# Two full-row phases per chunk instead of three in a fused scan and gated-unit kernel on TensorE

## The chip, the cores and the metric

The kernel runs on one core of a Trainium2 chip. The core has a matrix engine (TensorE, PE in the profile), a vector engine (VectorE, DVE), a scalar engine (ScalarE, ACT), a general one (GpSimd, POOL) and an engine that only issues transfers (SyncE, SP). The engines run side by side and wait for each other on semaphores. On each engine the instructions run in the order in which they were built. TensorE writes into PSUM, eight banks of 512 float32 columns on 128 partitions.

The metric is device time in microseconds (us) for one execution, the median of several runs. A profiled execution is a separate run with the hardware profiler on.

## The reference, cut to what matters

A layer norm of x (2048 tokens, 448 features) feeds two branches, whose product is added to x.

```python
xn = _layernorm(x)
# branch A: a diagonal complex recurrence over the 2048 tokens
dt = exp(log_dt);  Lam_bar = exp(dt * Lam)
B_bar = ((Lam_bar - 1.0) / Lam)[:, None] * Bmat
Bu = einsum("bld,pd->blp", xn, B_bar)
for t in range(L):
    h = Lam_bar * h + Bu[:, t, :]          # 448 complex states
y = 2.0 * einsum("blp,dp->bld", hseq, Cmat).real + xn * Dskip
# branch B: a gated unit, 448 -> 1792 -> 448
g = xn @ w_gate;  u = xn @ w_up
m = (sigmoid(g) * u) @ w_down
out = x + y * silu(m)
```

## The kernel before, in words

The tokens are cut into four chunks of 512, each of four tiles of 128. All weights stay on chip. For a chunk c the work is this:

- `prepare(c)`: normalize the four tiles on ScalarE (L456), turn them by transfers into the layout with features on partitions (`xnT`), and multiply the skip term on VectorE (`skip_row`, L464, into `xd`).
- 14 projection steps (`gu_step`): for each seventh of the hidden size one gate step ("g") and one up step ("u"). A step is seven pairs of half-row matmuls (L690, L691), each on 64 of the 128 rows of the array, 512 columns wide, and fills a buffer `gu` of two banks. There are three of them. ScalarE takes the tanh of a gate step out (L704, into `sig`, two buffers), and VectorE takes an up step out and multiplies (L707, into `hF`). The factor between tanh and sigmoid is put right later, by the scale of the Silu.
- Input projections of the recurrence (`b_units`): two groups, for scan parts 0 and 1, and 2 and 3. A group begins with half-row pairs, can put other work in (`mid`), and goes on with full-row matmuls (L758, L761). ScalarE copies the result into `bus` (L769 to L777).
- The recurrence (`whole(c)`): VectorE rotates the inputs, runs the scans (L812, L844) and rotates back into `hT`, one of two by parity of the chunk.
- `down(c, j)`: 14 full-row matmuls for tile j (L873) into one of two accumulator banks `acc`, and a Silu on ScalarE (L879) into one of six buffers `g_t`.
- `yout(c, j)`: seven full-row matmuls (L898) into an accumulator bank, then three operations on VectorE (L904 adds the skip term and frees the bank, L906 multiplies with `g_t`, L908 adds x), and the store (L910). The output buffers `o_t` are three, the `xd` buffers twelve.

`down` and `yout` take the two accumulator banks in turn.

Half-row and full-row matmuls are two modes of the array. A stretch of full-row work between half-row steps is called a phase here. Before the change chunks 2 and 3 have three: one in each group of input projections (the group's `down` goes between its half-row pairs and its full-row matmuls, and one `yout` follows), and a third with two `down` and two `yout` before the last two projection steps. Chunk 1 has three as well, without a `yout` in the first two. The `down` are of the chunk before. The `yout` in the third phase are of the chunk before, those in the first two of the chunk before that.

The order comes from a planner (`Plan`, L74). Every operation is recorded with an engine, an assumed duration in us and the names of what it reads and writes (`add`, L85). TensorE's operations stay in the order in which they are recorded, so the sequence from L922 to L1051 is TensorE's. For the other engines `solve` (L138) works back from TensorE's times to a latest start for each, then forward to a planned start, and `emit` (L240) issues everything in order of planned starts. The assumed durations thus set the order on VectorE, ScalarE, GpSimd and SyncE, and waits are made from the real dependences. The layer norm's inverse root for later tiles runs on GpSimd in `chain` (L425 to L446).

Behind the last projection step come the remaining `yout` and the four `down` of chunk 3, which use the free `gu` banks in place of accumulators.

Of the kernel before, what the change touches and what calls it, by code (L numbers as in the profile page):

```python
# [13 lines left out]
ALU = mybir.AluOpType  # L14
# [14 lines left out]
EPS = 1e-5  # L29
# [25 lines left out]
def dve1(n):  # L55
    return 0.067 + n / 960.0
# [17 lines left out]
class Plan:  # L74
# [10 lines left out]
    def add(self, eng, cost, fn, r=(), w=(), dma=0, lat=None, chain=False, name="", rate=230e3):  # L85
        o = Op()
        o.idx, o.eng, o.cost, o.fn, o.dma, o.name = len(self.ops), eng, cost, fn, dma, name
        o.lat = LAT.get(eng, 0.0) if lat is None else lat
        o.pre, o.suc, o.rate = {}, [], rate
        o.slot = None  # L90
        if dma and eng != "POOL":
            o.slot, self.n_dma = self.n_dma, self.n_dma + 1
        o.start = o.end = None
        for k in r:
            if k in self.w:
                self._edge(self.w[k], o, True)
        for k in w:
            for q in self.r.get(k, ()):
                self._edge(q, o, False)
            if k in self.w:  # L100
                self._edge(self.w[k], o, True)
        for k in w:
            self.w[k] = o
            self.r[k] = []
        for k in r:
            if k not in w:
                self.r.setdefault(k, []).append(o)
        if chain or eng == "PE" or (eng == "DVE" and self.seq):
# [137 lines left out]
def kernel(  # L246
# [18 lines left out]
    V, A, G, T, Q = nc.vector, nc.scalar, nc.gpsimd, nc.tensor, nc.sync  # L265
# [56 lines left out]
    mv = sbt("mv", [NT, 2])  # L322
# [22 lines left out]
    add = pl.add  # L345
# [80 lines left out]
    def chain(t0, n):  # L426
        ts = range(t0, t0 + n)
        var, mean = mv[:, t0:t0 + n, 1:2], mv[:, t0:t0 + n, 0:1]
        sd, rs, nm, ve = (q[:, t0:t0 + n, :] for q in (sdb, rsd, nmr, veb))
        ks = lambda k: [(k, t) for t in ts]  # L430
        if t0 < TPC:
            add("ACT", 0.3, lambda: A.activation(sd, var, ACT.Sqrt, bias=epsc[:]), r=ks("mv") + ["sqrttab", "epsc"], w=ks("sd"))
            add("POOL", 0.15, lambda: G.tensor_copy(out=meanf[:, t0:t0 + n, :], in_=mean), r=ks("mv"), w=ks("mf"))
            add("DVE", 0.2, lambda: V.reciprocal(out=rs, in_=sd), r=ks("sd"), w=ks("rs"))
            return
        bc = lambda t: t[:].unsqueeze(1).to_broadcast((P, n, 1))
        add("POOL", 0.4, lambda: G.tensor_single_scalar(out=ve, in_=var, scalar=EPS, op=ALU.add), r=ks("mv"), w=ks("ve"))
        add("POOL", 1.0, lambda: G.tensor_tensor(out=sd, in0=ve, in1=bc(halfc), op=ALU.pow), r=ks("ve") + ["consts"], w=ks("sd"))
        if t0 == TPC:
            add("DVE", 0.2, lambda: V.reciprocal(out=rs, in_=sd), r=ks("sd"), w=ks("rs"))  # L440
            add("DVE", 0.16, lambda: V.scalar_tensor_tensor(out=nm, in0=mean, scalar=-1.0, in1=rs, op0=ALU.mult, op1=ALU.mult),
                r=ks("mv") + ks("rs"), w=ks("nm"))
            return
        add("POOL", 1.0, lambda: G.tensor_tensor(out=rs, in0=sd, in1=bc(negc), op=ALU.pow), r=ks("sd") + ["consts"], w=ks("rs"))
        add("POOL", 0.4, lambda: G.tensor_tensor(out=nm, in0=mean, in1=rs, op=ALU.mult), r=ks("mv") + ks("rs"), w=ks("nm"))
        add("POOL", 0.4, lambda: G.tensor_single_scalar(out=nm, in_=nm, scalar=-1.0, op=ALU.mult), r=ks("nm"), w=ks("nm"))  # L446
# [419 lines left out]
    def down(c, j, first=False, bank=None):  # L866
        key, d = bank if bank else (lambda a: (("acc", a), acc[a][:, 0:D]))(next_acc())
        js = slice(j * P, j * P + P)

        def f():  # L870
            for ft in range(FT):
                m, h = ft % 7, ft // 7
                T.matmul(d, lhsT=hF[c % 2][:, m, h, js], rhs=wd[:, ft, :], start=(ft == 0), stop=(ft == FT - 1))  # L873
        add("PE", 14 * 0.189 + (SW if first else 0), f, r=[("wd", 0), ("wd", 1)] + [("hF", c % 2, m) for m in range(7)], w=[key],
            name=f"d{c}.{j}")
        g = gt_n[0] % NGT
        gt_n[0] += 1
        gt_of[c, j] = g
        add("ACT", act(448), lambda: A.activation(g_t[g][:], d, ACT.Silu, scale=0.5), r=[key, "silutab"], w=[("gt", g)])  # L879
# [4 lines left out]
    def yout(c, j, first=False, banks=None, parts=((0, D),)):  # L884
        js = slice(j * P, j * P + P)
        t = c * TPC + j
        g = gt_of[c, j]
        o = o_n[0] % NO
        o_n[0] += 1
        q = t % NXD  # L890
        xq = xd[q][:]
        for pi, (c0, c1) in enumerate(parts):
            key, y = banks[pi] if banks else (lambda a: (("acc", a), acc[a][:, 0:D]))(next_acc())
            y = y[:, 0:c1 - c0]

            def f(y=y, c0=c0, c1=c1):
                for i, (hm, cm) in enumerate(K_ORDER):
                    T.matmul(y, lhsT=hT[c % 2][:, hm, js], rhs=cT[:, cm, c0:c1], start=(i == 0), stop=(i == 6))  # L898
            n = c1 - c0
            add("PE", 7 * (0.004 + n / 2400.0) + (SW if first else 0), f,  # L900
                r=cTk + [("hT", c % 2, p) for p in range(4)], w=[key], name=f"y{c}.{j}")
            ok = ("o", o, pi)
            od = o_t[o][:, c0:c1]
            add("DVE", dve1(n), lambda od=od, y=y, c0=c0, c1=c1: V.tensor_tensor(out=od, in0=y, in1=xq[:, c0:c1], op=ALU.add),  # L904
                r=[key, ("xd", q)], w=[ok])
# [76 lines left out]
    one(1, 0, "u")  # L982
    prepare(2)
    b_units(1, (0, 1), lambda: down(0, 0, True))
    for i in range(3, 6):
        gu_step(1, i, i == 3)
    b_units(1, (2, 3), lambda: down(0, 1, True))
    for i in range(6, 12):
        gu_step(1, i, i == 6)
    down(0, 2, True)  # L990
    yout(0, 0)
    down(0, 3)
    yout(0, 1)
    for i in range(12, 14):
        gu_step(1, i, i == 12)
    whole(1)

    for i in range(0, 4):
        gu_step(2, i)
    b_units(2, (0, 1), lambda: down(1, 0, True))  # L1000
    yout(0, 2)
    for i in range(4, 7):
        gu_step(2, i, i == 4)
    b_units(2, (2, 3), lambda: down(1, 1, True))
    yout(0, 3)
    prepare(3)
    for i in range(7, 12):
        gu_step(2, i, i == 7)
    down(1, 2, True)
    yout(1, 0)  # L1010
    down(1, 3)
    yout(1, 1)
    for i in range(12, 14):
        gu_step(2, i, i == 12)
    whole(2)

    for i in range(0, 4):
        gu_step(3, i)
    b_units(3, (0, 1), lambda: down(2, 0, True))
    yout(1, 2)  # L1020
    for i in range(4, 7):
        gu_step(3, i, i == 4)
    b_units(3, (2, 3), lambda: down(2, 1, True))
    yout(1, 3)
    for i in range(7, 12):
        gu_step(3, i, i == 7)
    down(2, 2, True)
    yout(2, 0)
    down(2, 3)
    yout(2, 1)  # L1030
    for i in range(12, 14):
        gu_step(3, i, i == 12)
    whole(3)

    yout(2, 2, True)
    yout(2, 3)
    free_banks = []
    for s in range(3):
        a = (gu_n[0] + s) % 3
        for i in range(2):  # L1040
            free_banks.append((("gub", a, i), gu[a][:, i, 0:D]))
        gate([("gu", a)], [("gub", a, 0), ("gub", a, 1)])
    for j in range(2):
        down(3, j, bank=free_banks[j])
    for j in range(2):
        yout(3, j)
    down(3, 2, bank=free_banks[2])
    yout(3, 2)
    down(3, 3, bank=free_banks[3])
    a = next_acc()  # L1050
    yout(3, 3, banks=[(("acc", a), acc[a]), free_banks[4]], parts=((0, 128), (128, 448)))  # L1051
# [36 lines left out]
```

## Time and profile before

| what | value |
|---|---|
| median of 5 runs | 188.86 us (188.12 to 190.43) |
| profiled execution | 188.17 us |
| its span, first to last instruction | 186.4 us |
| TensorE clock granted | full in every slice |
| share of the span, chain that ended last | PE 60%, DVE 21%, DMA 8%, ACT 4% |
| u evacuations, L707 on `sig` | 21, mean 1214 ns |
| scans, L812 | 18 with a carried state, mean 1276 ns |
| L904 | 15 whole tiles, mean 615 ns |
| Silu, L879 | 16, mean 540 ns |
| moved by transfers over the span | 13.43 MB, mean 72 GB/s |

The profile is taken in one execution. Its own time is 1.77 us over its span. Matmuls are pipelined, and their ends are modelled, so for TensorE the distance between starts tells more than the durations: two rows overlap by the part that is hidden. On VectorE, too, a row overlaps the next by some 0.08 us. In a row, the text in brackets is the idle time just before it, and what ended it. A buffer's number is left out in names.

### The profile page before, as it was taken

The page shows a single profiled execution, that of the slowest core. Times are in us where ns is not written, and L with a number is a line of the kernel's source. Part 1 is how long each engine was busy: PE and PEld are TensorE (multiplying, and loading weights), DVE is VectorE, ACT ScalarE, POOL GpSimd, SP SyncE. Part 2 cuts the span into 40 slices and gives each one's busy share as a digit, 9 for nine tenths or more (in the row PEclk, how much of TensorE's full clock was granted, in tenths as well). Part 3 has the DMA queues.
Part 4 walks back from the last instruction along what each step waited for, and adds up shares of the span by engine and source line. Part 5 has one row for each costly group of instructions (what it writes and reads, how often), then busy time and mean ns, then how long its engine had stood idle before and what let it go on. Part 6 is the DMA issues. An engine that isn't in the chain of part 4 may idle for free.

```text
span 186.4 us, 3512 instructions
## 1 busy us (share of the span) xinstructions
PE 180.6 (97%) x1375; PEld 88.0 (47%) x1375; DVE 167.8 (90%) x303; ACT 87.7 (47%) x124; POOL 35.5 (19%) x87
## 2 busy tenths in 40 slices
PE   7999999999999999999999999999999999999991
PEld 2674444564444444444445445444445445445550
DVE  3732999999998999999999999999999999999963
ACT  3449997943949942241557441234444421501020
POOL 7135462920078000000048410000000000000000
PEclk9999999999999999999999999999999999999999
DMA  5999999499200038200000343000000000001220
GB/s 139 268 217 214 196 182 201 80 269 195 100 4 0 0 77 74 49 0 4 0 2 0 77 102 70 0 28 0 25 4 0 25 25 28 0 5 48 74 77 25
DMA packets 30257, 13.43 MB, mean 72 GB/s; under 512 B 19744, under 2 KB 30240, under 8 KB 30240
## 3 DMA queue, kind: packets, MB, share of 16 engines
q1 hardware_dynamic: 28336, 12.05, 32.0%
q10 hardware_dynamic: 1808, 1.15, 2.5%
q8 instruction: 11, 0.18, 0.4%
q14 instruction: 6, 0.05, 0.1%
q0 software_dynamic: 96, 0.00, 0.0%
HBM read 6.77 MB, written 1.84 MB: 46 GB/s over the span
## 4 chain that ended last, share of the span: by engine, by line
PE 60%; DVE 21%; DMA 8%; ACT 4%; issue 3%; POOL 1%; SPq 1%; DVEq 0%
PE gu L690 24%; PE acc L873 13%; PE acc L898 10%; PE gu L873 6%; DVE hF L707 6%; DMA x_all<-in_A_x_dram 5%; PE gu L758 4%; DMA wG<-in_B_w_gate_dram 3%; DVE bst L423 2%; DVE wv L812 2%; DVE cT L659 1%; DVE ta L805 1%; DVE ta L826 1%; SPq L351 1%; DVE tb L806 1%
## 5 line engine op out<-in xcount | busy, mean ns | idle before, releaser
L690 PE MATMUL gu<-xnT,wG 64*128 64x512 bf16 (+1 forms) x231 | 46.2, 344 | 0.3 <-DVE xnT L491 0.3
L691 PE MATMUL gu<-xnT,wG 64*128 64x512 bf16 (+1 forms) x231 | 46.2, 344 | 0.0
L690 PE MATMUL gu<-xnT,wU 64*128 64x512 bf16 x196 | 46.0, 376 | 0.0
L691 PE MATMUL gu<-xnT,wU 64*128 64x512 bf16 x196 | 46.0, 376 | 0.0
L704 ACT ACTIVATE sig<-gu 128x1024 f32<-128x1024 f32 x21 | 21.4, 1023 | 28.6 <-PE gu L691 24.2
L873 PE MATMUL acc<-wd,hF 128*128 128x448 bf16 x168 | 33.8, 353 | 0.2 <-ACT g_t L879 0.2
L873 PEld LDWEIGHTS <-hF 128*128 128x128 bf16 x224 | 21.2, 98 | 22.6 <-issue 3.9
L690 PEld LDWEIGHTS <-wG 64*128 64x128 bf16 x231 | 21.0, 94 | 21.2 <-issue 2.8
L690 PEld LDWEIGHTS <-wU 64*128 64x128 bf16 x196 | 18.1, 94 | 23.3 <-issue 1.4
L707 DVE SCALAR_TENSOR_TENSOR hF<-sig,gu 128x1024 bf16<-128x1024 f32 x21 | 25.5, 1214 | 2.5 <-PE gu L691 1.3
L812 DVE TENSOR_TENSOR_SCAN wv<-c_r,st,z 128x512 bf16<-128x512 f32 x18 | 23.0, 1276 | 0.0
L898 PE MATMUL acc<-cT,hT 128*128 128x448 bf16 (+1 forms) x112 | 22.6, 344 | 0.0
L691 PEld LDWEIGHTS <-wG 64*128 64x128 bf16 x231 | 21.0, 94 | 0.0
L879 ACT ACTIVATE g_t<-acc 128x448 bf16<-128x448 f32 x12 | 6.5, 539 | 28.5 <-PE acc L873 28.5
L691 PEld LDWEIGHTS <-wU 64*128 64x128 bf16 x196 | 18.1, 94 | 0.1
L758 PE MATMUL gu<-xnT,bT 128*128 128x512 bf16 x72 | 16.9, 379 | 0.0
L898 PEld LDWEIGHTS <-hT 128*128 128x128 bf16 x119 | 11.3, 98 | 10.0 <-issue 0.4
L423 DVE BATCH_NORM_STATS2 bst<-x_all 128x6 f32<-128x448 bf16 x16 | 9.4, 614 | 7.1 <-DMA x_all<-in_A_x_dram 7.1
L769 ACT CAST bus<-gu 128x1024 bf16<-128x1024 f32 x12 | 12.0, 1003 | 2.9 <-PE gu L758 2.8
L456 ACT ACTIVATE xn<-x_all,nmr,rsd 128x448 bf16<-128x448 bf16 x12 | 8.8, 768 | 7.3 <-DVE xd L464 4.6
L873 PE MATMUL gu<-wd,hF 128*128 128x448 bf16 x56 | 11.1, 352 | 0.0
L904 DVE TENSOR_TENSOR o_t<-acc,xd 128x448 bf16<-128x448 f32 (+1 forms) x16 | 9.5, 595 | 1.5 <-PE acc L898 1.4
(135 smaller groups left out, 240.8 us busy)
## 6 DMA issues: line engine op xcount, KB each, us to landing
out_dram<-o_t SPq DMA_DIRECT2D x15, 112.0 KB, 1.7
wd<-in_B_w_down_dram SPq DMA_DIRECT2D x2, 784.0 KB, 5.1
x_all<-in_A_x_dram SPq DMA_DIRECT2D x3, 448.0 KB, 5.2
wU<-in_B_w_up_dram SPq DMA_DIRECT2D x2, 448.0 KB, 11.9
wU<-in_B_w_up_dram SPq DMA_DIRECT2D x2, 336.0 KB, 7.2
wG<-in_B_w_gate_dram SPq DMA_DIRECT2D x2, 224.0 KB, 5.8
wG<-in_B_w_gate_dram ACTq DMA_DIRECT2D x2, 224.0 KB, 6.0
xnT<-xn SPq DMA_TRANSPOSE x24, 2.4
```

What stands on the lines that cost most here:

```text
L423: add("DVE", 0.6, lambda: V.bn_stats(out=bst[b][:], in_=x_all[:, t, :]), r=[("x", t)], w=[("bst", b)])
L456: add("ACT", 0.65, lambda: A.activation(xn[b][:, 0:448], x_all[:, t, :], ACT.Identity, bias=nmr[:, t, :], scale=rsd[:, t, :]), r=[("x", t) ...
L690: T.matmul(gu[a][:, 0, ts], lhsT=w_[0:H, s, ms], rhs=x[0:H, s, ts], start=(s == 0), stop=(s == 6))
L691: T.matmul(gu[a][:, 1, ts], lhsT=w_[H:P, (s + 1) % 7, ms], rhs=x[H:P, s, ts], start=(s == 0), stop=(s == 6))
L704: add("ACT", act(1024), lambda: A.activation(th, gu[a][:], ACT.Tanh, scale=0.5), r=[("gu", a)], w=[tk])
L707: add("DVE", dve1(1024), lambda: V.scalar_tensor_tensor(out=ho, in0=th, scalar=1.0, in1=gu[a][:], op0=ALU.add, op1=ALU.mult), r=[("gu", a) ...
L758: T.matmul(gu[a][:, i, :], lhsT=bT[:, kt, i, pt * P:pt * P + P], rhs=x[:, 2 * kt, :], start=False, stop=(kt == 2))
L769: add("ACT", act(1024), lambda u=u, a=a: A.copy(out=bus[u][:], in_=gu[a][:]), r=[("gu", a)], w=[("bus", u)])
L812: dve(1.194, lambda k=k: V.tensor_tensor_scan(out=wv[:, k, :], data0=rb, data1=z[:, k, :], initial=(st[pt][:, k, :] if c else 0.0), op0=AL ...
L873: T.matmul(d, lhsT=hF[c % 2][:, m, h, js], rhs=wd[:, ft, :], start=(ft == 0), stop=(ft == FT - 1))
L898: T.matmul(y, lhsT=hT[c % 2][:, hm, js], rhs=cT[:, cm, c0:c1], start=(i == 0), stop=(i == 6))
L904: add("DVE", dve1(n), lambda od=od, y=y, c0=c0, c1=c1: V.tensor_tensor(out=od, in0=y, in1=xq[:, c0:c1], op=ALU.add), r=[key, ("xd", q)], w ...
```

## The change

In chunk 1, the two phases of the input projections take two `down` of chunk 0 each, and there is no `yout`. In chunks 2 and 3 each of the two phases takes two `down` of the chunk before and two `yout` of the chunk before that, in turn. The third phase is gone, and so the last seven projection steps of a chunk follow each other. All `yout` of chunk 0 stand in chunk 2, all of chunk 1 in chunk 3, and all of chunk 2 behind the last projection step, where before there were two. There the `yout` of chunk 2 now alternate with `down` of chunk 3. In `chain` two assumed durations on GpSimd change. No operation's computation changes. The diff, with the removed repetition for chunk 3 left out:

```diff
-        add("POOL", 0.4, lambda: G.tensor_single_scalar(out=ve, in_=var, scalar=EPS, op=ALU.add), r=ks("mv"), w=ks("ve"))
-        add("POOL", 1.0, lambda: G.tensor_tensor(out=sd, in0=ve, in1=bc(halfc), op=ALU.pow), r=ks("ve") + ["consts"], w=ks("sd"))
+        add("POOL", 0.6, lambda: G.tensor_single_scalar(out=ve, in_=var, scalar=EPS, op=ALU.add), r=ks("mv"), w=ks("ve"))
+        add("POOL", 1.4 if n == 4 else 1.0, lambda: G.tensor_tensor(out=sd, in0=ve, in1=bc(halfc), op=ALU.pow), r=ks("ve") + ["consts"], w=ks("sd"))
...
     b_units(1, (0, 1), lambda: down(0, 0, True))
+    down(0, 1)
     for i in range(3, 6):
         gu_step(1, i, i == 3)
-    b_units(1, (2, 3), lambda: down(0, 1, True))
-    for i in range(6, 12):
+    b_units(1, (2, 3), lambda: down(0, 2, True))
+    down(0, 3)
+    for i in range(6, 14):
         gu_step(1, i, i == 6)
-    down(0, 2, True)
-    yout(0, 0)
-    down(0, 3)
-    yout(0, 1)
-    for i in range(12, 14):
-        gu_step(1, i, i == 12)
     whole(1)
-
-    for i in range(0, 4):
-        gu_step(2, i)
-    b_units(2, (0, 1), lambda: down(1, 0, True))
-    yout(0, 2)
-    for i in range(4, 7):
-        gu_step(2, i, i == 4)
-    b_units(2, (2, 3), lambda: down(1, 1, True))
-    yout(0, 3)
-    prepare(3)
-    for i in range(7, 12):
-        gu_step(2, i, i == 7)
-    down(1, 2, True)
-    yout(1, 0)
-    down(1, 3)
-    yout(1, 1)
-    for i in range(12, 14):
-        gu_step(2, i, i == 12)
-    whole(2)
...
+    for c in (2, 3):
+        for i in range(0, 4):
+            gu_step(c, i)
+        b_units(c, (0, 1), lambda: down(c - 1, 0, True))
+        yout(c - 2, 0)
+        down(c - 1, 1)
+        yout(c - 2, 1)
+        for i in range(4, 7):
+            gu_step(c, i, i == 4)
+        b_units(c, (2, 3), lambda: down(c - 1, 2, True))
+        yout(c - 2, 2)
+        down(c - 1, 3)
+        yout(c - 2, 3)
+        if c == 2:
+            prepare(3)
+        for i in range(7, 14):
+            gu_step(c, i, i == 7)
+        whole(c)
+
+    yout(2, 0, True)
     yout(2, 1)
-    for i in range(12, 14):
-        gu_step(3, i, i == 12)
-    whole(3)
-
-    yout(2, 2, True)
-    yout(2, 3)
...
-    for j in range(2):
-        down(3, j, bank=free_banks[j])
-    for j in range(2):
+    down(3, 0, bank=free_banks[0])
+    yout(2, 2)
+    down(3, 1, bank=free_banks[1])
+    yout(2, 3)
+    down(3, 2, bank=free_banks[2])
+    for j in range(3):
         yout(3, j)
-    down(3, 2, bank=free_banks[2])
-    yout(3, 2)
     down(3, 3, bank=free_banks[3])
```

More of the change, by code (lines that the diff above doesn't have):

```diff
@@ L984 @@
     b_units(1, (0, 1), lambda: down(0, 0, True))
+    down(0, 1)
     for i in range(3, 6):
         gu_step(1, i, i == 3)
-    b_units(1, (2, 3), lambda: down(0, 1, True))
-    for i in range(6, 12):
+    b_units(1, (2, 3), lambda: down(0, 2, True))
+    down(0, 3)
+    for i in range(6, 14):
         gu_step(1, i, i == 6)
-    down(0, 2, True)
-    yout(0, 0)
-    down(0, 3)
-    yout(0, 1)
-    for i in range(12, 14):
-        gu_step(1, i, i == 12)
-    whole(1)
-    for i in range(0, 4):
-        gu_step(2, i)
-    b_units(2, (0, 1), lambda: down(1, 0, True))
-    yout(0, 2)
-    for i in range(4, 7):
-        gu_step(2, i, i == 4)
-    b_units(2, (2, 3), lambda: down(1, 1, True))
-    yout(0, 3)
-    prepare(3)
-    for i in range(7, 12):
-        gu_step(2, i, i == 7)
-    down(1, 2, True)
-    yout(1, 0)
-    down(1, 3)
-    yout(1, 1)
-    for i in range(12, 14):
-        gu_step(2, i, i == 12)
-    whole(2)
[L1017 to L1029, printed above, removed]
-    yout(2, 1)
-    for i in range(12, 14):
-        gu_step(3, i, i == 12)
-    whole(3)
-    yout(2, 2, True)
-    yout(2, 3)
+    whole(1)
+    for c in (2, 3):
[17 more added lines that the diff above has]
+    yout(2, 0, True)
+    yout(2, 1)
     free_banks = []
```

## The prediction

> **What bounds the kernel now.** I read the engine shares of the page first, then TensorE's rows in order of time, then the waits, then VectorE's rows at the end. The shares alone leave two candidates:
>
> ```profile
> PE 180.6 (97%) x1375; PEld 88.0 (47%) x1375; DVE 167.8 (90%) x303; ACT 87.7 (47%) x124; POOL 35.5 (19%) x87
> ```
>
> Here a rule speaks against the change. The Trainium skill, "Perfetto Trace Analysis", Identifying the Most-Contended Engine, says that matmul busy time is no measure of how near TensorE is to its limit, while for VectorE the busy share is a fair one. By the rule alone VectorE (90%) would be the bound, and time taken off TensorE would be worth nothing. So I look at distances between starts instead. TensorE's timeline around the third full-row phase of chunk 2 (start, duration, engine, line; L690 and L691 are the two half-row matmuls of a pair, L873 is `down`, L898 is `yout`):
>
> ```profile
> 108.94 0.38 PE L690 MATMUL gu<-xnT,wU 64*128 64x512 bf16 x1
> 109.15 0.38 PE L690 MATMUL gu<-xnT,wU 64*128 64x512 bf16 x1
> 109.46 2.82 PE L873 MATMUL acc<-wd,hF 128*128 128x448 bf16 x14
> 112.12 1.49 PE L898 MATMUL acc<-cT,hT 128*128 128x448 bf16 x7
> 113.45 2.81 PE L873 MATMUL acc<-wd,hF 128*128 128x448 bf16 x14
> 116.09 1.49 PE L898 MATMUL acc<-cT,hT 128*128 128x448 bf16 x7
> 117.51 0.39 PE L690 MATMUL gu<-xnT,wG 64*128 64x512 bf16 x1
> ```
>
> Pairs start 0.215 us apart, so a projection step of seven pairs takes 1.51. A `down` takes 2.65, a `yout` 1.32. I laid these against every start from 75 us to the last matmul: there is no gap but the phase borders. The step before the phase takes 0.31 instead of 0.215 (109.15 to 109.46: 0.10 on entry), and the `yout` that ends it 1.42 instead of 1.33 (116.09 to 117.51: 0.09 on exit). So from 75 us on TensorE sets the end, the rule notwithstanding. The exception in chunk 1 is here:
>
> ```profile
> 68.76 1.49 PE L898 MATMUL acc<-cT,hT 128*128 128x448 bf16 x7
> 70.47 2.81 PE L873 MATMUL acc<-wd,hF 128*128 128x448 bf16 x14 [0.23 <-ACT g_t L879]
> ```
>
> This `yout` takes 1.71 to the next start where 1.32 is its due: 0.39 lost, because `down(0,3)` needs the accumulator whose Silu (L879) stands on ScalarE behind a normalization (L456) that waits for VectorE:
>
> ```profile
> 69.23 0.76 ACT L456 ACTIVATE xn<-x_all,nmr,rsd 128x448 bf16<-128x448 bf16 x1 [1.41 <-DVE xd L464]
> 69.90 0.52 ACT L879 ACTIVATE g_t<-acc 128x448 bf16<-128x448 f32 x1
> ```
>
> VectorE is nearly as full: the waits that end its idle time after 62 us are a few of 0.2 to 0.4, each for the up projection that it evacuates next. Its rows at the end show how much room there is:
>
> ```profile
> 163.80 1.22 DVE L707 SCALAR_TENSOR_TENSOR hF<-sig,gu 128x1024 bf16<-128x1024 f32 x1 [0.41 <-PE gu L691]
> 170.04 0.68 DVE L829 TENSOR_TENSOR hT<-ta,tb 128x1024 bf16<-128x1024 bf16 x1
> 175.57 0.62 DVE L904 TENSOR_TENSOR o_t<-acc,xd 128x448 bf16<-128x448 f32 x1
> 177.03 0.62 DVE L904 TENSOR_TENSOR o_t<-acc,xd 128x448 bf16<-128x448 f32 x1
> 181.44 0.29 DVE L904 TENSOR_TENSOR o_t<-acc,xd 128x128 bf16<-128x128 f32 x1 [1.41 <-PE acc L898]
> ```
>
> The last scan output `hT` of chunk 3 is ready at 170.72, and `yout(3,0)` starts at 171.57: 0.85 to spare. Before the last tile VectorE waits 1.41.
>
> **The change part by part.** *Borders.* Chunks 1, 2 and 3 lose one full-row phase each; the half-row pairs of the input projections already open the other two. Three entries and three exits go: 3 x (0.10 + 0.09) = 0.57, all on the path. The Trainium skill prices this differently: "TensorEngine Tiling (Array Packing)", Key Properties, says a change of tiling mode drains TensorE, and "TensorE: Matmul & The Clock Gate", Single matmul latency, gives a drain of roughly 175 ns. Six of those are 1.05. I take the rows, 0.57, and keep 1.05 for the range.
>
> *The lost 0.39 in chunk 1.* `yout(0,0)` and `yout(0,1)` leave chunk 1. The two accumulators then serve four `down` alone, each takes the one that the last but one `down` left, and at least a `down` (2.65) lies between, so the Silu (0.54) is done in time. The 0.39 goes. What is late next there: nothing on TensorE, since chunk 1 runs eight projection steps in a row, and of these only the u steps need VectorE.
>
> *The eight steps in a row* (twelve with the next chunk's first four). A slot of the three `gu` buffers must be free two steps (3.02) after its step ends, and a u evacuation takes 1.13 from start to start. I laid the built VectorE order end to end by the starts of the rows (scan 1.20, wide products and sums 0.60, L904 0.53, L906 and L908 0.30, L464 0.30), from the first u evacuation of chunk 1 at 41.99, which stands in the same place. Chunk 1's next ones then fall 0 to 0.4 after their steps end; VectorE waits for TensorE there, not the other way. In chunks 2 and 3 a few stand behind scans and are 1.0 to 1.5 later, inside the 3.02, or, beside the input projections, later still but before the slot's turn. One place has only 1.5: the u step two before the second input projection. There VectorE arrives within 0.5 of the step's end in both chunks, as it did before (row at 137.10, slot taken at 138.33). Cost nothing; the cover is some 1 us of VectorE lead, and what exceeds it comes at full price.
>
> *`yout` a chunk later.* The scan output may now be up to a phase later, so VectorE's scans get slack; against that, `down` and `yout` alternate on two accumulators in both phases, and L904 must free one within the 2.65 of the `down` between. In my lay-out L904 is at its place at 87.5 for a `yout` that ends at 87.4, and at 102.4 and 130.2 VectorE waits for it: margin 2.0. The two stores that moved on SP's queue behind six transposes keep none waiting: the output buffer they free is wanted some 5 us later. ScalarE's Silu of `down(1,3)` waits on its queue for L906 of `yout(0,1)`, some 12 us after its matmuls; behind it stands the next chunk's first tanh, which has its input only then. Nothing.
>
> *POOL's planned costs* (0.6 and 1.4 for 0.4 and 1.0) change no instruction, only places: VectorE takes the reciprocal L440, on which it idled 0.32, after a second L562, and L634 goes ahead of the third u evacuation. TensorE lost 0.33 at the first input projection (29.35; 0.76 to the next start where 0.43 is due), waiting for the fifth u evacuation that ended at 29.74; laid out anew it ends at 29.1. But L634 needs a transfer that POOL's copies saw land near 24.9, just when it is its turn, and the table step behind follows later. Bounds: 0.33 gained, 0.3 lost; I take 0.15 gained, as the larger of the two effects is off TensorE.
>
> *The tail.* Two more `yout` stand behind the last projection step: before `yout(3,0)` TensorE now has four `yout` and three `down`, 4 x 1.32 + 3 x 2.65 = 13.2. VectorE, from the last u evacuation on: 1.13, two scans 2.40, eight wide operations 4.83, L859 0.33, two L904 1.06, three L464 0.90, seven L906/L908 2.15, together 12.8, and 0.53 for the L904 that frees `yout(3,0)`'s accumulator, 13.3, and some 0.2 of latency at both ends. So `yout(3,0)` waits about 0.2: the 0.85 to spare is gone. From there VectorE needs 1.75, then 2.8 with the L904 of `yout(3,0)` in it, then two tiles of 1.46 (175.57 to 177.03), and reaches the last tile 20.8 after the last projection step; TensorE, with three `yout` and a `down` and the 0.60 from its end to L904 (180.84 to 181.44), also 20.8. The 1.41 is gone too, but nothing more is lost.
>
> Sum: -0.57 - 0.39 - 0.15 + 0.2 = -0.9. The profiled execution took 188.17, its span of 186.4 and 1.77 around it, so 187.3 for its like. It stands 0.69 under the median of 188.86; carried to the median, 188.0.
>
> **The rivals.** *VectorE is the bound after all.* Its work is the same and 0.9 less room leaves it no slack, so the end stays: 188.9. For it: 90% busy and the two margins that vanish. Against: the lay-out, where it waits 3 to 5 us in all for TensorE before the tail. *Slower: accumulators starve TensorE.* Where VectorE is more than 2.0 late at the L904 between two `yout`, TensorE stands. Two such places in chunk 2, two in chunk 3 and the one before `yout(3,0)`: at one scan (1.2) too late in three of them, 3.6 - 0.9 = +2.7, 191.6. For it: VectorE's order is fixed by a plan whose costs are not those of the rows, so one late transfer shifts all behind it. Against: it decides only from 2.0 late, and the old order, with three such places, had no such wait. *More is gained:* the drain at the skill's 1.05, 0.39 and 0.33, with no wait at the tail, 1.77, and the spread of the runs on top: 186.9. *That it isn't done:* TensorE's order is the program's own, and the built one has two phases a chunk; excluded.
>
> **How the numbers follow.** Forecast, 188.0: 0.60. VectorE bound, 188.9: 0.12. Slower, 191.6: 0.16, nearly all past 190.75. More gained, 186.9: 0.12, taken as past 1%. About 1% is what a measurement of this kernel can tell from no change, as its five runs spread over 2.3 us. So faster 0.12, same 0.72, slower 0.16. The forecast's own range is 187.1 (1.77 gained) to 188.6 (switch saved, tail 0.5 worse). To leave out no more than 2 in 10 it reaches to 186.9 below and, past the bound case, to 190.0 above.
>
> **What would show it.** Right: TensorE's rows have two full-row stretches in chunks 1 to 3, borders of 0.10 and 0.09 each; no wait for L879 near 66 us; the last projection step ends 3.6 us earlier than 163.6; `yout(3,0)` starts near 173, within 0.5 of the last L829. Wrong: rows of `yout` or `down` that start more than 0.3 after the step before, with L904 as releaser; a projection step that waits for L707; a bus copy (L769) late behind a normalization on ScalarE; or the scans of chunk 3 ending after 174.

## The result, and the profile after

The changed kernel takes 187.77 us in the median (187.14 to 188.52), the kernel before 188.51 in the runs beside it. The ratio is 0.9963, with a 95% interval of 0.9951 to 0.9976. That is 0.70 us less (the two medians stand 0.74 apart); the prediction had 188.0 against 188.86, a ratio of 0.9955.

The engine shares of the page hardly move, and the span, first to last instruction, goes from 186.4 to 186.0. The profiled execution itself did not get shorter: it took 188.52, the slowest of the 36, with 2.52 outside its span where the one before had 1.77. In the runs of the kernel before beside the experiments the time outside the span is always 1.72 to 1.95. In the changed kernel it is above 2.1 in 6 of 36, up to 2.90. No instruction stands in that time, and what takes it is not shown. So what follows, which is read from traces, is about the span alone.

What did move is the page's chain that ended last. The page's engine shares, then the chain's shares of the span by engine and by line:

```profile
PE 180.0 (97%) x1375; PEld 88.6 (48%) x1375; DVE 167.9 (90%) x303; ACT 87.8 (47%) x124; POOL 34.9 (19%) x87
...
DVE 4%; issue 1%; DVEq 0%
DVE o_t L904 2%; DVE o_t L906 1%; DVE xd L464 1%; DVE o_t L908 1%; DVEq L906 0%
```

Before, this chain was 60% TensorE. Now, followed back from the last instruction, it stays on VectorE. It ends after some 5% of the span and says nothing on what held TensorE before that, so it is a statement on the tail alone.

TensorE's timeline of the changed kernel, at the end of the second phase of chunk 1 and at the end of the second phase of chunk 2:

```profile
59.44 2.81 PE L873 MATMUL acc<-wd,hF 128*128 128x448 bf16 x14
62.18 0.39 PE L690 MATMUL gu<-xnT,wG 64*128 64x512 bf16 x1
...
105.04 1.49 PE L898 MATMUL acc<-cT,hT 128*128 128x448 bf16 x7
106.46 0.39 PE L690 MATMUL gu<-xnT,wU 64*128 64x512 bf16 x1
```

The `down` takes 2.74 to the next start, 2.65 and the 0.09 of a border. The `yout` takes 1.42, 1.33 and 0.09. Behind each, the half-row steps follow at 1.51 without a gap. Behind the first there are twelve in a row, from 62.18 to 80.32, at the place where chunk 1 had its third phase and its 0.39 of waiting.

The tail has changed sides. TensorE's timeline, then VectorE's, with the idle time before a row in brackets:

```profile
170.50 2.81 PE L873 MATMUL gu<-wd,hF 128*128 128x448 bf16 x14
173.47 4.13 PE L898 MATMUL acc<-cT,hT 128*128 128x448 bf16 x21 [0.16 <-DVE o_t L904]
177.44 2.81 PE L873 MATMUL gu<-wd,hF 128*128 128x448 bf16 x14
180.09 0.55 PE L898 MATMUL acc<-cT,hT 128*128 128x128 bf16 x7
```

```profile
172.21 0.68 DVE L829 TENSOR_TENSOR hT<-ta,tb 128x1024 bf16<-128x1024 bf16 x1
172.81 0.61 DVE L904 TENSOR_TENSOR o_t<-acc,xd 128x448 bf16<-128x448 f32 x1
173.34 0.38 DVE L464 TENSOR_TENSOR xd<-xn,dbc 128x448 bf16<-128x448 bf16 x1
173.81 0.62 DVE L904 TENSOR_TENSOR o_t<-acc,xd 128x448 bf16<-128x448 f32 x1
...
178.27 0.62 DVE L904 TENSOR_TENSOR o_t<-acc,xd 128x448 bf16<-128x448 f32 x1
...
179.73 0.62 DVE L904 TENSOR_TENSOR o_t<-acc,xd 128x448 bf16<-128x448 f32 x1
180.45 0.39 DVE L906 TENSOR_TENSOR o_t<-o_t,g_t 128x448 bf16<-128x448 bf16 x1
180.87 0.39 DVE L908 TENSOR_TENSOR o_t<-o_t,x_all 128x448 bf16<-128x448 bf16 x1
181.18 0.28 DVE L904 TENSOR_TENSOR o_t<-acc,xd 128x128 bf16<-128x128 f32 x1
...
182.85 0.32 DVE L908 TENSOR_TENSOR o_t<-o_t,x_all 128x320 bf16<-128x320 bf16 x1
```

The `down` at 170.50 takes 2.97 to the next start instead of 2.65. The accumulator of `yout(3,0)` comes free with the L904 that starts at 172.81 and ends at 173.42, so 0.32 is lost. Its `hT` was ready at 172.89, before TensorE would have come to it (173.15). And the last tile's L904 at 181.18 has no idle time before it. Before, VectorE waited 1.41 for TensorE there; now the matmuls are there first.

The two profiled executions, cut into stretches by starts on TensorE, with the end of the last L908:

| stretch | before | after | difference |
|---|---|---|---|
| to the first projection step | 7.92 | 8.11 | +0.19 |
| to the first half-row pair of chunk 1's input projections | 33.47 | 33.23 | -0.24 |
| to the end of the last projection step | 122.23 | 118.56 | -3.67 |
| to the narrow `yout` of the last tile | 17.22 | 20.19 | +2.97 |
| to the end of the last L908 | 2.76 | 3.08 | +0.32 |

Two `yout` (2.65) went from the third row to the fourth. Without them the third lost 1.02, and the fourth gained 0.32. All together is -0.43, and -0.62 without the first row. The ratio, which holds many executions, says -0.70.

### The profile page after: what moved, and what is told of

It is laid out like the page before. It is cut to its first block, busy times and chain, and to the rows that moved or that the text cites. A ratio compares the mean times of both kernels' runs of the same rounds, so it can differ in the third digit from the quotient of the medians.

```text
span 186.0 us, 3513 instructions
## 1 busy us (share of the span) xinstructions
PE 180.0 (97%) x1375; PEld 88.6 (48%) x1375; DVE 167.9 (90%) x303; ACT 87.8 (47%) x124; POOL 34.9 (19%) x87
## 5 line engine op out<-in xcount | busy, mean ns | idle before, releaser
L690 PEld LDWEIGHTS <-wG 64*128 64x128 bf16 x231 | 21.3, 94 | 20.9 <-issue 1.9
L707 DVE SCALAR_TENSOR_TENSOR hF<-sig,gu 128x1024 bf16<-128x1024 f32 x21 | 25.5, 1216 | 2.7 <-PE gu L691 2.0
L812 DVE TENSOR_TENSOR_SCAN wv<-c_r,st,z 128x512 bf16<-128x512 f32 x18 | 23.0, 1277 | 0.0
L691 PEld LDWEIGHTS <-wG 64*128 64x128 bf16 x231 | 21.2, 94 | 0.0
L879 ACT ACTIVATE g_t<-acc 128x448 bf16<-128x448 f32 x12 | 6.5, 538 | 26.1 <-PE acc L873 16.7
L423 DVE BATCH_NORM_STATS2 bst<-x_all 128x6 f32<-128x448 bf16 x16 | 9.3, 612 | 5.5 <-DMA x_all<-in_A_x_dram 5.5
L758 PEld LDWEIGHTS <-bT 128*128 128x128 bf16 x72 | 6.9, 98 | 8.5 <-issue 0.7
L437 POOL TENSOR_SCALAR veb<-mv 128x2 bf16<-128x2 bf16 (+1 forms) x5 | 2.5, 503 | 43.3 <-DVE mv L424 43.3
```

What stands on the lines that cost most here:

```text
L423: add("DVE", 0.6, lambda: V.bn_stats(out=bst[b][:], in_=x_all[:, t, :]), r=[("x", t)], w=[("bst", b)])
L690: T.matmul(gu[a][:, 0, ts], lhsT=w_[0:H, s, ms], rhs=x[0:H, s, ts], start=(s == 0), stop=(s == 6))
L691: T.matmul(gu[a][:, 1, ts], lhsT=w_[H:P, (s + 1) % 7, ms], rhs=x[H:P, s, ts], start=(s == 0), stop=(s == 6))
L707: add("DVE", dve1(1024), lambda: V.scalar_tensor_tensor(out=ho, in0=th, scalar=1.0, in1=gu[a][:], op0=ALU.add, op1=ALU.mult), r=[("gu", a) ...
L758: T.matmul(gu[a][:, i, :], lhsT=bT[:, kt, i, pt * P:pt * P + P], rhs=x[:, 2 * kt, :], start=False, stop=(kt == 2))
L812: dve(1.194, lambda k=k: V.tensor_tensor_scan(out=wv[:, k, :], data0=rb, data1=z[:, k, :], initial=(st[pt][:, k, :] if c else 0.0), op0=AL ...
```

## The experiments

All ratios are to the kernel before, which ran beside each. The changed kernel's own 0.9963 is what the variants of it are held against. A difference of 0.002 in the ratio is 0.38 us.

**The phases without the edit of the assumed durations, and the edit without the phases.** The first is the changed kernel with:

```diff
-        add("POOL", 0.6, ...
-        add("POOL", 1.4 if n == 4 else 1.0, ...
+        add("POOL", 0.4, ...
+        add("POOL", 1.0, ...
```

> The changed kernel with the old planned costs on GpSimd. Theory (TensorE sets the end up to the last projection step; the gain is 0.57 for six borders and 0.39 for the Silu wait): the borders and the Silu wait stay gone, only the 0.23 us at the first input projection may come back, so 0.4 to 0.8 us under the kernel before. Rival (the gain comes from the new places that the planned costs give in the first 40 us): no gain over the kernel before.

Measured: 188.19 us, ratio 0.9994 (0.9970 to 1.0018). The point lies outside what was expected (0.9957 to 0.9979); the interval reaches into it. The second is the kernel before with the new numbers.

> The kernel before with the new planned costs alone. Theory: at most the 0.33 us wait at the first input projection goes, so 0 to 0.3 us under the kernel before, with all three phases and their borders in place. Rival (planned costs): the whole gain, some 0.7 us.

Measured: 188.25 us, ratio 0.9996 (0.9976 to 1.0015). So neither half shows a gain by itself, while both together do, though the intervals of the first half and of the whole change touch. The traces suggest why. In the first, TensorE's stretch from the first pair of chunk 1 to the narrow `yout` is 138.77, as in the changed kernel (138.75; 139.45 before), and the end behind it is 3.10, also as there (3.08; 2.76 before). But TensorE reaches chunk 1's first pair 34.06 after the first projection step, where the changed kernel needs 33.23 and the kernel before 33.47. TensorE's timeline of this variant at the first input projection:

```profile
29.13 0.38 PE L743 MATMUL gu<-xnT,bT 64*128 64x512 bf16 x1
29.81 0.37 PE L743 MATMUL gu<-xnT,bT 64*128 64x512 bf16 x1 [0.30 <-DVE hF L707]
30.14 2.12 PE L758 MATMUL gu<-xnT,bT 128*128 128x512 bf16 x9
```

The second pair waits for an evacuation, L707, and 1.01 pass to the full-row matmuls where 0.53 is due (two pairs at 0.215 and the entry of 0.10). In the second variant the same place takes 1.12, while the wait for the Silu in chunk 1 is gone without any change of phases there, because VectorE and ScalarE are planned anew.

**The front of the new plan with the back of the old one.** To tell whether those 0.4 were lost in front, the order of all engines up to the first input projection was taken from the changed kernel's plan, and everything behind it from the plan with the old durations:

```diff
     pl.solve({"g0.0": 5.9})
+    T0 = next(o.start for o in pl.ops if o.name == "bp0.0") + 0.1
+    first = {o.idx: o.start for o in pl.ops if o.start < T0}
+    for o, cost in recost:
+        o.cost = cost
...
+    pl.solve({"g0.0": 5.9})
+    for o in pl.ops:
+        o.start = first[o.idx] if o.idx in first else o.start + 1000.0
```

> The phases of the change, with the order of all engines taken from the plan with the new GpSimd costs up to the first input projection, and from the plan with the old costs behind it. It differs from the phases with the old costs alone (ratio 0.9994) only in VectorE's, ScalarE's and GpSimd's order ahead of 30 us. If the 0.42 by which that one stood above the changed kernel was lost in front of the first input projection, this one is at the changed kernel's 0.996. If it was lost behind it, or by chance of the runs, it stays at 0.999.

Measured: 187.83 us, ratio 0.9973 (0.9950 to 0.9996). It lies between the two, nearer to the changed kernel; its interval holds both. In its trace the first input projection takes the due 0.53, and chunk 1's first pair comes 33.34 after the first projection step. But in that execution the load of chunk 1's x tiles also landed earlier than in the one with the old durations (tables at the end), so this trace alone does not tell the order from the landing. The time leans to the front and does not settle it.

**The Silu's wait, taken out another way.** The kernel before, with the third phase of chunk 1 as `down`, `down`, `yout`, `yout`:

```diff
     down(0, 2, True)
-    yout(0, 0)
     down(0, 3)
+    yout(0, 0)
     yout(0, 1)
```

> The kernel before, with the third phase of chunk 1 in the order down, down, yout, yout in place of down, yout, down, yout: same work, same borders, but the Silu that frees the accumulator has 2.65 us in place of 1.32. Theory: the 0.39 us wait at 70 us goes and the end comes 0.4 us earlier, since from there on TensorE has no gap. Rival (VectorE is the bound): TensorE's wait goes and the end stays.

Measured: 189.11 us, ratio 1.0031 (1.0017 to 1.0045): slower. The wait went, as expected; the two `down` now take 5.31, twice 2.65. But no gain came, which neither the theory nor its rival had; the planner had moved VectorE's order everywhere, and the trace shows new waits. TensorE's timeline of this variant:

```profile
30.88 0.37 PE L743 MATMUL gu<-xnT,bT 64*128 64x512 bf16 x1 [0.96 <-DVE hF L707]
...
62.55 0.37 PE L690 MATMUL gu<-xnT,wG 64*128 64x512 bf16 x1 [0.21 <-ACT bus L777]
```

The row at 62.55 is a projection step that waits for a copy on ScalarE (0.37 by distances), where there was none, and from chunk 1's first pair to the narrow `yout` the stretch is 139.45 as before. In this trace a wait's gain was taken out behind 40 us and put back by another one there. The row at 30.88 is no fair sample: this execution took 190.38, 1.27 over its median, and the load of the x tiles landed late in it (tables at the end). Part of the wait is the new order's, and what the 0.6 of the medians is made of is not shown.

**More borders.** In chunks 2 and 3 one projection step goes into the middle of each phase of the changed kernel:

```diff
         yout(c - 2, 0)
-        down(c - 1, 1)
+        gu_step(c, 4, True)
+        down(c - 1, 1, True)
         yout(c - 2, 1)
...
```

> The changed kernel with one projection step set between the first yout of each phase of chunks 2 and 3 and the down behind it: same work, four full-row phases per chunk in place of two, so four more pairs of borders. Theory: four times 0.19, 0.76 us over the changed kernel, so level with the kernel before. Rival (VectorE is the bound): as the changed kernel, 0.7 us under the kernel before.

Measured: 188.68 us, ratio 1.0006 (0.9987 to 1.0024): 0.8 us over the changed kernel, level with the one before. In its trace every added `yout` takes 1.42 and every added step 1.61. From chunk 1's first pair to the narrow `yout` it is 139.28; the changed kernel's 138.75 without its wait of 0.32 is 138.43. So eight more borders cost 0.85 on TensorE, where the rows' price of 4 x (0.10 + 0.09) is 0.76. The 0.8 of the time is another matter, and that it meets the 0.76 is luck as far as the trace goes. There VectorE had caught up when the tail began: `yout(3,0)` does not wait, and the tail from the last projection step to the end of the last L908 is 22.63, 0.64 shorter than the changed kernel's 23.27. So 0.21 of the 0.85 is left at the end. The rest of what this execution lost, 0.95, was lost before chunk 1's first pair (34.18 after the first projection step against 33.23), where the load of the x tiles landed later and VectorE's order is another.

**Two more VectorE copies in the tail.** The same two copies of 0.30 were put behind the L904 of `yout(2,3)`, in both kernels:

```diff
-            add("DVE", dve1(n), lambda ...: V.tensor_tensor(out=od, in0=y, in1=xq[:, c0:c1], op=ALU.add),
+            add("DVE", dve1(n), lambda ...: (V.tensor_tensor(out=od, in0=y, in1=xq[:, c0:c1], op=ALU.add),
+                V.tensor_copy(out=ctmp[0][:], in_=spm[:, 0, 0, 0:448]) if (c, j) == (2, 3) else None,
+                V.tensor_copy(out=ctmp[1][:], in_=spm[:, 0, 1, 0:448]) if (c, j) == (2, 3) else None),
```

> The kernel before with two extra copies on VectorE (some 0.3 us each) behind the L904 of the last tile of chunk 2, with results that nobody reads. Theory: VectorE waits 1.41 us before the last tile there, so the 0.6 us are hidden and the time is that of the kernel before. Rival (VectorE is the bound): 0.6 us more.

> The changed kernel with the same two extra copies at the same place. Theory: VectorE has no idle time left behind that place, so the full 0.6 us: level with the kernel before or 0.1 under. Rival (TensorE holds the end): 0.7 us under the kernel before, as the changed kernel.

Measured: in the kernel before 188.79 us, ratio 0.9997 (0.9968 to 1.0025), and in the changed one 188.28 us, ratio 0.9988 (0.9967 to 1.0010), 0.5 over the changed kernel. VectorE's timeline of the first, and TensorE's of the second:

```profile
182.94 0.29 DVE L904 TENSOR_TENSOR o_t<-acc,xd 128x128 bf16<-128x128 f32 x1 [0.81 <-PE acc L898]
```

```profile
174.40 2.81 PE L898 MATMUL acc<-cT,hT 128*128 128x448 bf16 x14 [0.16 <-DVE o_t L904]
177.57 1.49 PE L898 MATMUL acc<-cT,hT 128*128 128x448 bf16 x7 [0.37 <-DVE o_t L904]
```

Before, the 0.60 came out of the 1.41 of idle time: 0.81 is left, and from the last projection step to the end of the last tile it is 19.98, to the hundredth what it was without the copies. In the changed kernel `yout(3,2)` waits for VectorE, and the same stretch is 23.87 against 23.27: the whole 0.60. Of all traces this pair says most plainly that the bound of the tail has changed. The times agree with it and do not prove it, since the interval of the second touches the changed kernel's.

**Four skip products less.** The skip products of the last four tiles are left out of the changed kernel, so the outputs of chunk 3 are made with the skip term of chunk 0:

```diff
-        add("DVE", dve2(448), lambda: V.tensor_tensor(out=xd[q][:], ...),
+        add("DVE", dve2(448), lambda: V.tensor_tensor(out=xd[q][:], ...) if t < 12 else None,
```

> The changed kernel without the skip product of the last four tiles (four L464 of 0.30 us on VectorE, three of them behind the last scan output; leaves out that part of the computation: the tiles of chunk 3 read the skip term of chunk 0), all else at its place. Theory (the tail is now VectorE's by 0.3 to 0.5 us): the end comes 0.4 to 0.5 us before the changed kernel's, then TensorE holds it; 1.1 to 1.2 us under the kernel before. Rival (VectorE is the bound all along): the full 1.2 us, 1.9 under. Rival (TensorE holds the end): nothing more than the changed kernel, 0.7 under.

Measured: 187.11 us, ratio 0.9897 (0.9852 to 0.9941). VectorE's timeline of it:

```profile
180.17 0.29 DVE L904 TENSOR_TENSOR o_t<-acc,xd 128x128 bf16<-128x128 f32 x1 [0.63 <-PE acc L898]
```

VectorE waits for TensorE again, and the tail is 22.95 from the last projection step to the end of the last L908, against 23.27: the 0.32 of the table's last row. The wait of `yout(3,0)` stays at 0.31, since the products left out come behind it. The time is another matter. The ratio, 1.9 us under the kernel before, is better than the trace can explain; by itself it is what the rival had, for which VectorE is the bound all along. But it comes from six runs, and its interval reaches from 1.1 to 2.8 us under the kernel before, so that the theory's 1.1 to 1.2 lies at its edge. In the trace, where VectorE waits at the end and only 0.32 is gained, it is the theory that holds.

**The products of chunks 2 and 3 on GpSimd.**

```diff
+        if t < 8:
             add("DVE", dve2(448), lambda: V.tensor_tensor(out=xd[q][:], ...),
+        else:
+            add("POOL", 1.1, lambda: G.tensor_tensor(out=xd[q][:], ...),
```

> The changed kernel with the skip product of chunks 2 and 3 (eight L464) on GpSimd in place of VectorE. Theory: 2.4 us less on VectorE, five of the eight behind the last projection step, so both the wait of yout(3,0) of 0.3 us and the 0.4 us at the end go: 1.3 to 1.4 us under the kernel before. Rival: GpSimd takes over 2 us for one or slows VectorE's two-input operations beside it, and nothing is gained over the changed kernel.

Measured: 190.08 us, ratio 1.0083 (1.0057 to 1.0108): slower. The tail did what was wanted: 19.88 from the last projection step to the narrow `yout`, without a wait. But that step ended at 162.20 instead of 159.90. GpSimd's, VectorE's and TensorE's timelines of this variant around 60 to 70 us (its lines are numbered four higher: L468 is the product, L816 the scan, L812 the sum of two products, L711 the evacuation):

```profile
59.19 2.00 POOL L468 TENSOR_TENSOR xd<-xn,dbc 128x448 bf16<-128x448 bf16 x1
...
63.94 3.39 POOL L468 TENSOR_TENSOR xd<-xn,dbc 128x448 bf16<-128x448 bf16 x2
```

```profile
60.28 1.45 DVE L812 TENSOR_TENSOR z<-ta,tb 128x1024 bf16<-128x1024 bf16 x1
...
64.45 2.05 DVE L816 TENSOR_TENSOR_SCAN wv<-c_r,z 128x512 bf16<-128x512 f32 x1
...
67.87 0.68 DVE L812 TENSOR_TENSOR z<-ta,tb 128x1024 bf16<-128x1024 bf16 x1
```

```profile
69.74 0.37 PE L694 MATMUL gu<-xnT,wG 64*128 64x512 bf16 x1 [1.44 <-DVE hF L711]
```

A product takes GpSimd 1.2 to 2.3, and beside it some of VectorE's operations stretch: a sum takes 1.45, and 0.68 when GpSimd is idle (67.87), and a scan 2.05 instead of 1.21. The Trainium skill, "SBUF — State Buffer", SBUF: two separate sides, says that the two engines share a pair of ports, and that a VectorE operation with two inputs in SBUF and a GpSimd operation that reads SBUF exclude each other. The stretched rows are of that kind. So the evacuation came late (the four stretched rows before it are 3.2 over their usual durations, more than the 1.6 that TensorE lost there), the projection step before it took 3.11 instead of 1.51, and a step at 111 and the pairs of the input projections at 140.7 lost 0.39 each.

**Four products of chunk 2 moved to where VectorE is idle.** Same instructions, same engine, and the planned starts of four of them set by hand:

```diff
     pl.solve({"g0.0": 5.9})
+    for t, u in ((8, (2, 0)), (9, (2, 0)), (10, (2, 2)), (11, (2, 2))):
+        skip_op[t].start = u_op[u].start - 0.001
```

> The changed kernel with one thing moved: the four skip products (L464) of chunk 2 stand ahead of two u evacuations of chunk 2 (near 77.6 and 94.8 us) at which VectorE was idle 0.60 and 0.64 waiting for TensorE, instead of in the tail. The order of everything else is the changed kernel's. If the tail is VectorE's now, 1.2 us leave it: yout(3,0) starts without the 0.32 of waiting, and the last tile's L904 waits for TensorE again; the stretch from the end of the last projection step to the end of the last L908 becomes 22.5 instead of 23.27, and the ratio to the kernel before about 0.992 (0.990 to 0.994). If VectorE had no real room at those two places, a projection step near 79 or 96 waits for L707 and the gain is given back: 0.996.

Measured: 187.54 us, ratio 0.9955 (0.9936 to 0.9975). VectorE's timeline at the first of the two places and in the tail:

```profile
77.17 0.69 DVE L464 TENSOR_TENSOR xd<-xn,dbc 128x448 bf16<-128x448 bf16 x2
77.85 1.22 DVE L707 SCALAR_TENSOR_TENSOR hF<-sig,gu 128x1024 bf16<-128x1024 f32 x1
...
174.95 0.62 DVE L904 TENSOR_TENSOR o_t<-acc,xd 128x448 bf16<-128x448 f32 x1 [0.60 <-PE acc L898]
```

The 0.60 for which VectorE had been idle before that evacuation in the changed kernel (77.58) is filled, no projection step behind it became late, and `yout(3,0)` starts without a wait. The tail is 22.63, 0.64 shorter than the changed kernel's 23.27. That is what was expected (22.5), within 0.13. The time is not: the median is only 0.23 lower, and the interval reaches past no gain. By the spans it is 0.35 lower (medians 185.45 and 185.80): here too the time outside the span is above 2.1 in 6 of 22 executions, and that is not in the tail's account.

**The x tiles of chunk 1 loaded earlier**, alone and with the moved products:

```diff
     pl.solve({"g0.0": 5.9})
+    x4_op.start = u0_op.start - 0.001
```

> The changed kernel with one transfer moved on SP's queue: the load of x tiles 4 to 7 goes ahead of the first two loads of wU instead of behind them; the order on every compute engine is the changed kernel's. If the wait at the first input projection (0.10 to 1.25 over the profiles) comes from the landing of these tiles, L423 starts at 15 or earlier, the wait is 0.1 or less in the profile, and the median falls by what the wait costs on average, 0.3 to 0.6: ratio 0.993 to 0.995. If it comes from VectorE's own order, nothing changes: 0.996. If wU's first block, now 2 us later, misses the first u projection step at 20.3, that step waits up to 1 us and the kernel is slower: 0.998 to 1.002.

> Both moves at once, the skip products of chunk 2 and the load of x tiles 4 to 7, in the changed kernel. They touch the two ends of the kernel, so their gains should add: 0.988 to 0.991 if both theories hold, about 0.992 if only the tail's does.

Measured: alone 187.70 us, ratio 0.9961 (0.9941 to 0.9981), with the products 187.31 us, ratio 0.9936 (0.9916 to 0.9955). The tiles are taken up at 13.9 and 13.5, and the first input projection takes the due 0.52 and 0.53 in both. But alone it changes nothing in the median. In the profiled executions the wait goes with the landing (tables at the end); whether ordinary executions have that wait is not shown. The two together are the fastest complete kernel here, 0.46 under the changed one by the medians. In the trace its last L908 ends 0.58 earlier, counted from the first projection step (174.48 against 175.06). The ratio falls short even of the 0.992 that was expected if the tail's theory alone holds, though the interval reaches to it.

## Why the prediction was right, step by step

The time fell within 0.3 us of the forecast, and the likeliest case was the one that came: TensorE's path got shorter by the borders and the Silu's wait, and the tail gave some of it back to VectorE. The terms did less well than their sum.

- **Borders, -0.57: right.** Each stretch that begins or ends half-row work shows 0.09 to 0.10, and more borders cost 0.85 for a priced 0.76. The drain at 1.05 is excluded: the stretch that holds borders and Silu lost 1.02 in all.
- **The Silu's wait, -0.39: right for this change.** No wait for L879 is left. Borders and Silu make 0.96 of the 1.02. But the term is not a property of the phases. It also goes when only the assumed durations change (1.33 for that `yout`), and where it was taken out by itself another wait came.
- **The eight and twelve steps in a row, nothing: right.** They follow each other at 1.51.
- **`yout` a chunk later, nothing: right.** The L904 that was forecast at 87.5 is at 87.66, and VectorE waits at 102.6 and 130.4, as laid out. The starving accumulators of the slower rival came only in the tail.
- **The planned costs, -0.15: mis-read, and the size was luck.** The trace shows -0.24 in front. Its upper bound, 0.33, held 0.10 for the phase's entry, which follows that pair and does not go. And it is no constant: with the same order on VectorE five traces lose nothing at that place and two lose 0.84 and 1.10, with the landing of a transfer (tables at the end). The step took this edit for a trifle beside the phases. Without it the phases did not measure as a gain.
- **`yout(3,0)` waits 0.2: the mechanism right, the size 0.32.** It started at 173.47, 0.58 after the end of the last L829 (172.21 and 0.68), where the prediction gave 0.5. The prediction's own terms make 0.3 (13.3 and 0.2 of latency against 13.2), which it put down as 0.2.
- **"The 1.41 is gone too, but nothing more is lost": wrong.** This is the step that failed. VectorE was to be at the last tile 20.8 after the last projection step, level with TensorE. It was there after 21.28 (159.90 to 181.18), while TensorE, with its 0.60, was at 20.79. Of the 0.49 between, 0.16 came back within the last tile, whose second part had waited for TensorE before (L908 at 182.09, L904 at 182.39) and waits no more (181.83, 181.97); the rest is the last row of the table.

What was missing stands in two places. The 20.8 is 13.3 + 1.75 + 2.8 + 2 x 1.46, and the latency that the prediction counted for `yout(3,0)` is not in it: VectorE was through with the L904 at 13.44 (173.34), not at 13.3. And from there to the last two tiles (178.27) it took 4.93, where the prediction had 1.75 + 2.8 = 4.55. In that stretch four operations read the result of the one right before them. Three L908 start 0.42 behind their L906, where the lay-out's price is 0.30, and one L904 starts 0.47 behind its L464 (173.34 to 173.81), also for 0.30. That is 0.53, more than the 0.38 that were missing, so part of it must have been in the prediction's two sums. It had the distances between dependent rows in full for the last two tiles, in their 1.46, and these came out right. The four products left out and the four moved both bring the lost time back in the trace.

So the forecast was 0.9, and the trace gives -0.57 - 0.39 - 0.06 (spread over the rest of that stretch) - 0.24 + 0.32 + 0.32 = -0.62 from the first projection step on. The front gave 0.09 more than priced, and the tail took 0.44 more. The rival "VectorE is the bound after all" was true in the tail, which is the last 23 us, and in this trace there alone.

Two things stay open. One is how far front waits of ordinary executions agree with profiled ones, since the landing is known for one execution of each kernel. So the account above is shown for traces, and how the 0.70 of the ratio divides between phases and assumed durations is not. The other is the time outside the span. In the seven kernels whose VectorE does not wait before the last tile (the changed one; changed with old durations, with two copies more, with the new front and old back, with the products moved, with x early, and with both moves), it is above 2.1 in 28 of 152 executions, up to 3.07. In the six variants where VectorE does wait there, it is in none of 99. That is a coincidence of two things in the record, not a cause shown. It may be one reason why the moved products are worth 0.64 in the trace, but 0.23 and 0.39 by the medians (187.77 to 187.54, 187.70 to 187.31).

## What to carry to other kernels

When time comes off one engine, lay the end of the kernel out for the next one row by row, with the distance from each instruction to the one that reads its result, not with one price for all. Where a planner sets the order from assumed durations, no edit is local: price it from the new order of every engine, and test it with the order held fixed and only the one thing moved. Where a load's landing differs from one execution to the next, compare two orders only at like landings. A wait that was taken away in such a kernel is a gain only when the whole timeline is checked for the one that took its place.

## What the runs showed of the hardware

A VectorE operation that reads the result of the one right before it starts later. VectorE's timeline of the changed kernel:

```profile
176.21 0.39 DVE L906 TENSOR_TENSOR o_t<-o_t,g_t 128x448 bf16<-128x448 bf16 x1
176.63 0.39 DVE L908 TENSOR_TENSOR o_t<-o_t,x_all 128x448 bf16<-128x448 bf16 x1
176.94 0.38 DVE L906 TENSOR_TENSOR o_t<-o_t,g_t 128x448 bf16<-128x448 bf16 x1
```

From L906 to the L908 of the same tile are 0.42, from that L908 to another tile's L906 0.31, with the same duration in the rows: 0.11 to 0.12 for the dependence. From the L464 at 173.34 to the L904 that reads its product are 0.47, and 0.30 from an L464 to an operation that does not read it: 0.17.

The wait at the first input projection follows the landing of one transfer. L423 is the first work on the x tiles of chunk 1. The first table has the traces with the changed kernel's order of VectorE at this place. Both columns count from the first projection step of 512 columns (14.44 in the changed kernel). "Late" is how much later than in the changed kernel the pair behind the first full-row matmuls starts (L743, 18.33 there).

| kernel | L423 starts | late |
|---|---|---|
| both moves | -0.29 | 0 |
| x early | -0.19 | 0 |
| changed | 1.77 | 0 |
| new front, old back | 2.02 | 0 |
| four products left out | 2.93 | 0 |
| four products moved | 4.40 | 0.84 |
| two copies more | 4.66 | 1.10 |

Up to 2.93 the landing is covered. The two late ones lie 0.26 apart in both columns: there lateness costs its full price, and the cover, reckoned back from these two, ends at 3.56. Other orders of VectorE have less of it. The differences of the two columns:

| order | L423 starts | late | difference |
|---|---|---|---|
| kernel before | 2.96 | 0.23 | 2.73 |
| the same, two copies more in the tail | 3.89 | 1.28 | 2.61 |
| more borders | 3.30 | 0.91 | 2.39 |
| products on GpSimd, with the same order there | 2.93 | 0.53 | 2.40 |
| changed, old durations | 3.51 | 0.47 | 3.04 |
| before, third phase of chunk 1 as `down`, `down`, `yout`, `yout` | 4.65 | 2.83 | 1.82 |

So at a landing of 3.5 the changed kernel's order would lose nothing, the old durations lose 0.47, and the kernel before would lose some 0.8: an estimate from these rows. Each of these numbers comes from one execution. In the first table's five without a moved load L423 started between 16.2 and 18.8, with nothing edited ahead of it.
